# Row writes moved half a unit behind their transposes, and a unit's four loads issued together

## The chip, the cores and the metric

The kernel runs on one core of a Trainium2 chip. What counts is the device time of one execution in microseconds (us). Three timed runs of the kernel before gave 659.62, 659.68 and 662.8 us, so the median is 659.68 us.

## The reference: retention attention, then a mixture of experts

The inputs q, k and v have 8 batches, 8 heads, 576 positions and 64 values per head. The first half of the work is an attention without a softmax, whose scores decay with the distance of the two positions:

```
scores = matmul(q, k^T) / sqrt(64)
Dmat[i, j] = gamma_h ** (i - j) if i >= j else 0      # gamma_h = 1 - 2**(-5-h)
x = matmul(scores * Dmat, v)                          # 4608 tokens x 512
```

The second half routes the 4608 tokens to 8 experts. All token and expert logits (x @ w_gate) are sorted together, and the list is walked from the largest: a token goes to an expert that still has room, and an expert takes 576 tokens. Each expert then computes `relu(x @ w1[e]) @ w2[e]` for its own tokens.

## The kernel before

**Attention in 16 units.** A unit is one batch pair `bp` (4 of them) and one head pair `hp` (4 of them). Unit `u = 4*bp + hp` has 9 blocks of 128 positions, counted by a running step `g = 9*u + blk`. The loop at L769 works a unit in two halves, the first with blocks 0 to 3 and the second with 4 to 8. A half calls, in this order: `ahead(g)` for its blocks, the score matmuls of the next half (`A`, L551, with the mask multiply `am` on VectorE, L566), the state and value matmuls (`across`, `ST`, `within`), the eviction of the result to `xT` (`evict`, L628 on VectorE), and last the fills of its blocks, `fills(gs)`.

**Loads.** Each unit needs four tiles: `kin` and `qin` (k and q transposed), `vin` (v) and `nin` (k as it is). `load` (L505) issues them from the SP queue (L516). Each of the four names has three buffers, so the loads of unit u+2 need the buffers of unit u-1 free: k waits for TensorE's last score matmuls of unit u-1, q for the `across` matmuls at its end. The SP queue works in order: a DMA at its head that waits holds up everything behind it. `ahead` (L749) calls `load` for unit u+2.

**Scaling of v.** `vscale` (L543, L546) multiplies `vin` by powers of gamma in place on GpSimd (POOL), with two instructions for each unit, 512 and 640 columns wide. In the program it comes one unit ahead. POOL has nothing else to do in the attention, so it works as soon as a `vin` has landed.

**Fills.** What has to be done for a finished batch pair while the next one runs hangs on steps, by `at(g, f, ...)`: the router's logits (`logits`, `logits2`), the counts of the first search (`count_first`: tiles m, t, mx, oh and G on VectorE; `first_digits`: om, dg, DF and D; `first_table`: FT), and the copy of the attention's rows to the DRAM tensor `xd`, from which the experts' tokens are gathered later. For the first three batch pairs that copy is `rows` (L660): one VectorE transpose for each of 9 blocks (L665) into a tile `xr` that holds three blocks and has two buffers. After the third block of a tile four DMAs write it to `xd` (L670). The fourth batch pair's rows go another way (`rows_pe`, L685).

**After the attention.** The expert part begins with a search over the logits on VectorE and TensorE, then takes eight experts in turn. All of it hangs on the end of the attention.

Of the kernel before, what the change touches and what calls it, by code (L numbers as in the profile page):

```python
# [19 lines left out]
NP, HP, NB = 4, 4, 9  # L20
# [477 lines left out]
def attention(tc, nc, P, qk, vk, cst_d, wg_d, rf, xd, Lg):  # L498
# [6 lines left out]
    def load(u, what, cuts=None):  # L505

        bp, hp = divmod(u, HP)
        for i in what:
            n = 1024 if i == "n" else 1152
            t = P['ld'].tile([128, n], F32, name=i + "in", bufs=3)  # L510
            src = qk[bp, hp, "qk".index(i)] if i in "qk" else vk[bp, hp, :, :1152] if i == "v" else vk[bp, hp, :, 1152:]
            LD[u, i] = t
            if cuts:
                pieces[u, i] = [(t[:, a:b], src[:, a:b]) for a, b in zip((0,) + cuts, cuts + (n,))]
            else:
                nc.sync.dma_start(t, src)  # L516
# [19 lines left out]
    G = 16*NB  # L536
# [6 lines left out]
    def vscale(u, a, b):  # L543

        v = LD[u, 'v'][:, 128*a:128*b].rearrange("p (a d) -> p a d", d=64)
        nc.gpsimd.tensor_tensor(v, v, vs[:, u % HP, 2*a:2*b, None].to_broadcast([128, 2*(b-a), 64]), op=ALU.mult)  # L546
# [86 lines left out]
    def bank(shape, name):  # L633
        turn[0] += 1
        return P['bank'](tags[turn[0] % len(tags)], shape, name)
# [19 lines left out]
        c0 = bp*NB + b0  # L655
        nc.vector.tensor_reduce(Lg[:, c0:c0+n, :], pt[:, :n, :, 0:8].rearrange("p j h e -> p j e h"), axis=AX.X, op=ALU.add)

    TR = {}

    def rows(bp, blk):  # L660

        j = blk % 3
        if j == 0:
            TR[0] = P['w'].tile([128, 12, HP, 32], F32, name="xr", bufs=2)
        nc.vector.transpose(TR[0][:, 4*j:4*j+4].rearrange("p b h i -> p h b i"),  # L665
                            XT[bp][:, :, blk*128:(blk+1)*128].rearrange("p h (b i) -> p h b i", i=32))
        if j == 2:
            o = (bp*NB + blk - 2)*128
            for a in range(4):
                nc.sync.dma_start(xd[o:o+384, 128*a:128*a+128].rearrange("(b j) c -> j b c", j=32),  # L670
                                  TR[0][32*a:32*a+32].rearrange("p b h i -> p b (h i)"))

    def rows_pe(bp, blk, hps=range(HP)):

        if 0 in hps:
            TR[1] = bank([128, 512], "pT")
        pt = TR[1]
        for hp in hps:
# [18 lines left out]
    def at(g, f, *a):  # L697
        fill.setdefault(g, []).append((f, a))

    def rest(it):  # L700
        for _ in it:
            pass
    def both(a, b):
        while True:
            x, y = next(a, 0), next(b, 0)
            if x == y == 0:
                return
            yield
# [3 lines left out]
    for bp in range(NP):  # L712
        g0 = (bp+1)*4*NB + 2
        for k, b0 in enumerate((0, 3, 6)):
            if bp == NP-1 and k == 2:
                break
            g1 = g0 + 6*k if bp < NP-1 else G - NB + b0 + 3 + (1 if k == 0 else 0)
            c0 = bp*NB + b0
            at(g1, logits, bp, b0, b0+3)
            at(g1+4 if bp < NP-1 else g1+(1 if k == 0 else 2), logits2, bp, b0, b0+3)  # L720
            if bp == NP-1:
                it = R.count_first(c0, c0+3)
                if k == 0:
                    for i in range(6):
                        at(g1+2+i//2, next, it, None)
                else:
                    at(G-1, lambda it, k: rest(both(it, R.first_digits(27, 30) if k else iter(()))), it, k)
            elif k == 2:
                it = R.count_first(9*bp, 9*bp+9)
                for i in range(8):  # L730
                    at(g1+5+i//2, next, it, None)
                at(g1+13, lambda bp: R.count_first_pe([9*bp, 9*bp+3, 9*bp+6], bank), bp)
        if bp < NP-1:
            for blk in range(NB):
                at(g0 + (12 if bp < NP-2 else 10)*(blk//3) + 2*(blk%3) + 4, rows, bp, blk)
    for bp in range(3):
        g0, it = (bp+1)*4*NB + 2, R.first_digits(9*bp, 9*bp+9)
        for i in range(10):
# [10 lines left out]
    def ahead(g):  # L749

        u, blk = divmod(g, NB)
        if u + 2 < 16:
            if blk == 3:
                load(u + 2, "kq")
            if blk == 5:
                load(u + 2, "v")
            if blk == 6:
                load(u + 2, "n")
        if u + 1 < 16:
            if blk == 2:  # L760
                vscale(u + 1, 0, 4)
            if blk == 5:
                vscale(u + 1, 4, 9)
# [5 lines left out]
    for u in range(16):  # L769
        for hf in range(2):  # L770
            gs = range(NB*u + 4*hf, NB*u + 4 + 5*hf)
            for g in gs:
                ahead(g)
            if hf == 0 and u % HP == 0:
                XT[u//HP] = P['xt'].tile([128, HP, 1152], F32, name="xT")
            A(u + hf, 1 - hf)
            if hf == 0:
                A2(u)
            PX[u, hf] = two.tile([128, 2, 512], F32, name="pX", tag="X", bufs=1)
            across(u, (2, 3) if hf else (1,))  # L780
            ST(u, 1 + 2*hf)
            if u == 15 and hf:
                fills(gs[:1])
                gs = gs[1:]
            within(u, hf)
            ST(u + hf, 2 - 2*hf)
            if hf:
                within2(u)
                across(u, (4,))
            for c0, c1 in ((2, 3), (3, 4)) if u == 15 and hf else ((2*hf, 2*hf + 2),):  # L790
                evict(u, c0, c1)
            if hf:
                evict(u, 4, 5)
            fills(gs)
    P['close']()
    P['open']("pb")
    bp = NP-1
# [14 lines left out]
    c = R.first_digits(30, 36)  # L812
# [245 lines left out]
def build(tc, nc, qk, vk, cst, wg, rf, w1, w2, out):  # L1058
    with ExitStack() as top:
# [32 lines left out]
        with ExitStack() as ctx:  # L1092
            Q = dict(P)
            for name, bufs in (("a", 1), ("ld", 2), ("w", 2), ("xt", 2)):
                Q[name] = ctx.enter_context(tc.tile_pool(name="a_" + name, bufs=bufs))
            R, rows = attention(tc, nc, Q, qk, vk, cst, wg, rf, xd, Lg)

            def idle(what):

                if what in ("row", "rows"):  # L1100
                    if rows:
                        rows.pop(0)()
                    else:
                        warm(1)
                    what = 2*(what == "rows")
                if what:
                    warm(what)
            R.idle = idle
            run = moe(tc, nc, P, R, xd, w1, w2, out, mix)
            mix.drain(lambda: 0 in run.regs)  # L1110
            while rows:
                rows.pop(0)()
# [20 lines left out]
```

## Time and profile before

| what | value |
|---|---|
| median of three timed runs | 659.68 us |
| the profiled execution's own time | 656.27 us |
| its span, first to last instruction | 654.5 us |
| TensorE busy | 610.3 us (93%) |
| VectorE busy | 415.7 us (64%) |
| GpSimd busy | 179.2 us (27%) |
| mean granted TensorE clock | 0.987 of full speed |

The profile is of one execution. The span is its time between the first and the last instruction; the 1.8 us between it and 656.27 us lie around it. A busy share is an average over the whole span: the attention fills about the first 150 us of it, and the experts the rest. An idle time in brackets, as [2.30 <-DVE am L566], is how long the engine stood before the row and what released it. A row that begins with a time and has x2 or x4 is of so many instructions merged.

### The profile page before, as it was taken

The page shows a single profiled execution, that of the slowest core. Times are in us where ns is not written, and L with a number is a line of the kernel's source. Part 1 is how long each engine was busy: PE and PEld are TensorE (multiplying, and loading weights), DVE is VectorE, ACT ScalarE, POOL GpSimd, SP SyncE. Part 2 cuts the span into 40 slices and gives each one's busy share as a digit, 9 for nine tenths or more (in the row PEclk, how much of TensorE's full clock was granted, in tenths as well). Part 3 has the DMA queues.
Part 4 walks back from the last instruction along what each step waited for, and adds up shares of the span by engine and source line. Part 5 has one row for each costly group of instructions (what it writes and reads, how often), then busy time and mean ns, then how long its engine had stood idle before and what let it go on. Part 6 is the DMA issues. An engine that isn't in the chain of part 4 may idle for free.

```text
span 654.5 us, 14685 instructions
## 1 busy us (share of the span) xinstructions
PE 610.3 (93%) x5756; PEld 519.8 (79%) x5756; DVE 415.7 (64%) x1504; ACT 244.8 (37%) x424; POOL 179.2 (27%) x221
## 2 busy tenths in 40 slices
PE   8799897978868999999999999999999999999995
PEld 6677776765458877987997798789779889988984
DVE  3487969798855987887896799588774302311300
ACT  1111111113254344553455156235615734653511
POOL 2341122210221135134143141332314135131111
PEclk9999898999997999999999999999999999999999
DMA  9997898954379359789499568928966895893521
GB/s 337 401 388 230 270 344 272 335 174 146 129 192 219 67 187 248 177 233 240 136 227 230 167 161 209 242 89 204 227 191 155 188 277 153 195 244 117 98 64 40
DMA packets 51702, 134.19 MB, mean 205 GB/s; under 512 B 5810, under 2 KB 19762, under 8 KB 51634
## 3 DMA queue, kind: packets, MB, share of 16 engines
q1 hardware_dynamic: 36530, 81.08, 36.2%
q0 software_dynamic: 14960, 51.91, 35.9%
q8 instruction: 45, 0.74, 0.4%
q10 hardware_dynamic: 144, 0.26, 0.1%
q14 instruction: 23, 0.19, 0.1%
HBM read 81.33 MB, written 18.87 MB: 153 GB/s over the span
## 4 chain that ended last, share of the span: by engine, by line
PE 68%; DVE 15%; DMA 8%; issue 5%; ACT 1%; POOL 1%; SPq 1%; POOLq 0%; DVEq 0%; ACTq 0%
PE ph L961 26%; PE py L1000 24%; PE pA L564 4%; DMA qin<-in_qk 3%; PE pX L608 3%; PE pS L587 2%; PE pX L599 2%; DMA w1l<-raw 2%; PE pt L932 2%; PE r L332 2%; DMA w2l<-raw 1%; PE pT L641 1%; DMA cst<-in_cst 1%; DVE xr L665 1%; DVE am L566 1%
## 5 line engine op out<-in xcount | busy, mean ns | idle before, releaser
L1000 PE MATMUL py<-w2h,hb 128*128 128x512 f32 x576 | 188.2, 399 | 0.0
L961 PE MATMUL ph<-xh,w1l 128*128 128x320 f32 (+1 forms) x512 | 150.7, 298 | 6.0 <-DMA w1l<-raw 6.0
L961 PE MATMUL ph<-xh,w1h 128*128 128x320 f32 (+1 forms) x512 | 153.3, 303 | 2.5 <-ACT xh L934 1.8
L961 PE MATMUL ph<-xl,w1h 128*128 128x320 f32 (+1 forms) x512 | 150.6, 298 | 0.0
L1000 PE MATMUL py<-w2l,hb 128*128 128x512 f32 (+1 forms) x320 | 125.4, 392 | 0.2 <-DMA w2l<-raw 0.2
L1000 PEld LDWEIGHTS py<-w2h,hb 128*128 128x128 f32 x576 | 104.0, 188 | 20.6
L961 PEld LDWEIGHTS ph<-xh,w1l 128*128 128x128 f32 x512 | 97.4, 192 | 6.2 <-DMA w1l<-raw 6.2
L961 PEld LDWEIGHTS ph<-xh,w1h 128*128 128x128 f32 x512 | 97.3, 191 | 4.5 <-ACT xh L934 2.7
L961 PEld LDWEIGHTS ph<-xl,w1h 128*128 128x128 f32 x512 | 97.5, 192 | 0.6 <-DVE cs L336 0.3
L968 DVE SCALAR_TENSOR_TENSOR hb<-ph,hb 128x256 fp32r<-128x256 f32 (+1 forms) x192 | 59.1, 352 | 56.0 <-ACT hb L965 55.3
L965 ACT ACTIVATE hb<-ph 128x256 fp32r<-128x256 f32 (+1 forms) x128 | 52.4, 409 | 107.3 <-PE ph L961 107.3
L977 POOL DMA_INDIRECT out_y<-yt,idx x40 | 41.2, 1030 | 118.7 <-ACT yt L1017 76.6
L1000 PEld LDWEIGHTS py<-w2l,hb 128*128 128x128 f32 (+1 forms) x320 | 56.7, 177 | 13.8 <-DMA w2l<-raw 1.2
L546 POOL TENSOR_TENSOR vin<-vin,cst 128x512 f32<-128x512 f32 (+1 forms) x32 | 37.3, 1183 | 100.3 <-DMA vin<-in_vk 76.5
L906 POOL DMA_DIRECT2D w2l<-raw x32 | 28.9, 902 | 122.5 <-ACT hb L965 116.2
L589 ACT ACTIVATE S<-pS 128x128 f32<-128x128 f32 x64 | 17.8, 278 | 114.8 <-PE pS L587 114.8
L917 POOL DMA_INDIRECT xg<-xd,idx x40 | 41.5, 1037 | 70.3 <-DMA raw<-in_w 37.1
L1017 ACT ACTIVATE yt<-py 128x512 f32<-128x512 f32 x32 | 19.2, 598 | 105.8 <-PE py L1000 79.9
L564 PE MATMUL pA<-qin,kin 64*128 64x128 f32 x512 | 38.5, 289 | 13.4 <-DVE am L566 9.7
L566 DVE TENSOR_TENSOR am<-pA,cst 128x1024 f32<-128x1024 f32 x32 | 39.0, 1220 | 18.5 <-PE pA L564 18.3
L564 PEld LDWEIGHTS pA<-qin,kin 64*128 64x128 f32 x512 | 32.2, 191 | 22.8 <-DVE am L566 11.8
L1020 DVE TENSOR_TENSOR yt<-yt,py 64x512 f32<-64x512 f32 x8 | 5.4, 679 | 69.6 <-ACT yt L1019 69.5
(177 smaller groups left out, 889.9 us busy)
## 6 DMA issues: line engine op xcount, KB each, us to landing
raw<-in_w SPq DMA_DIRECT2D x64, 512.0 KB, 5.4
w2l<-raw POOLq DMA_DIRECT2D x32, 512.0 KB, 5.5
w1l<-raw POOLq DMA_DIRECT2D x31, 512.0 KB, 7.2
kin<-in_qk SPq DMA_DIRECT2D x14, 576.0 KB, 8.0
qin<-in_qk SPq DMA_DIRECT2D x14, 576.0 KB, 7.7
vin<-in_vk SPq DMA_DIRECT2D x14, 576.0 KB, 7.8
nin<-in_vk SPq DMA_DIRECT2D x14, 512.0 KB, 8.4
xd<-xr SPq DMA_DIRECT2D x36, 192.0 KB, 3.6
```

The source lines that it names most:

```text
L546: nc.gpsimd.tensor_tensor(v, v, vs[:, u % HP, 2*a:2*b, None].to_broadcast([128, 2*(b-a), 64]), op=ALU.mult)
L564: nc.tensor.matmul(pa[:, r, j], LD[u, 'k'][half(r), s], LD[u, 'q'][half(r), s], start=True, stop=True, skip_group_check=True)
L566: nc.vector.tensor_tensor(AM[u, hf], pa, m1[:, None, None, :].to_broadcast([128, 2, 4, 128]), op=ALU.mult)
L608: nc.tensor.matmul(PX[u, hf][half(h), b, 128*c:128*c+128], v[:, a:a+64], AM[u, hf][:, h ^ b, j], start=False, stop=False, skip_group_check ...
L906: nc.gpsimd.dma_start(lo, raw, accum_op=ALU.add)
L917: nc.gpsimd.indirect_dma_start(out=xg[:n, j, :], out_offset=None, in_=xd[:, :], in_offset=bass.IndirectOffsetOnAxis(ap=found[e][:n, j:j+1] ...
L961: T.matmul(ps, w, x, start=(k == 0), stop=(k == 11))
L965: A.activation(hb[:, f, c], ps, AF.Relu)
L968: V.scalar_tensor_tensor(hb[:, f, to+a:to+b], ps[:, a:b], 0.0, hb[:, f, 256*s+a:256*s+b].bitcast(F32), op0=ALU.max, op1=ALU.subtract)
L977: st = nc.gpsimd.indirect_dma_start(out=out[:, :], out_offset=bass.IndirectOffsetOnAxis(ap=found[e][:n, t:t+1], axis=0), in_=y[:n], in_off ...
L1000: T.matmul(ps[:m], a, w, start=(k == 0), stop=(k == last), skip_group_check=True)
L1017: A.activation(y, ps, AF.Copy)
```

## The change

The four DMAs that write a tile `xr` become a function of their own, `store`, hung six steps behind the tile's last transpose (and no later than the attention's last step). `ahead` issues all four loads of unit u+2 at a unit's first block, where it issued k and q at block 3, v at block 5 and n at block 6. `vscale` stays on GpSimd, at the steps where it was.

```diff
-    TR = {}
+    TR, TD = {}, {}
...
-        if j == 2:
-            o = (bp*NB + blk - 2)*128
-            for a in range(4):
-                nc.sync.dma_start(xd[o:o+384, 128*a:128*a+128].rearrange("(b j) c -> j b c", j=32),
-                                  TR[0][32*a:32*a+32].rearrange("p b h i -> p b (h i)"))
+        TD[bp, blk//3] = TR[0]
+
+    def store(bp, k):
+
+        o = (bp*NB + 3*k)*128
+        for a in range(4):
+            nc.sync.dma_start(xd[o:o+384, 128*a:128*a+128].rearrange("(b j) c -> j b c", j=32),
+                              TD[bp, k][32*a:32*a+32].rearrange("p b h i -> p b (h i)"))
...
-                at(g0 + (12 if bp < NP-2 else 10)*(blk//3) + 2*(blk%3) + 4, rows, bp, blk)
+                g1 = g0 + (12 if bp < NP-2 else 10)*(blk//3) + 2*(blk%3) + 4
+                at(g1, rows, bp, blk)
+                if blk % 3 == 2:
+                    at(min(g1 + 6, G - 1), store, bp, blk//3)
...
-        if u + 2 < 16:
-            if blk == 3:
-                load(u + 2, "kq")
-            if blk == 5:
-                load(u + 2, "v")
-            if blk == 6:
-                load(u + 2, "n")
+        if blk == 0 and u + 2 < 16:
+            load(u + 2, "kqvn")
```

Only the SP queue's order changes. On it, everything up to the q load of unit 7 stands as before. The first place is the SP queue around the first two row writes, those of batch pair 0. Before, with vin_817, vin_946 and vin_1079 (the next) the v tiles of units 7, 8 and 9:

```order
L516 DMA kin_759<-in_qk 128x1152
L516 DMA qin_761<-in_qk 128x1152
L670 DMA xd_65<-xr_748 32x12x128 x4
L516 DMA vin_817<-in_vk 128x1152
L516 DMA nin_820<-in_vk 128x1024
L516 DMA kin_880<-in_qk 128x1152
L516 DMA qin_882<-in_qk 128x1152
L516 DMA vin_946<-in_vk 128x1152
L516 DMA nin_949<-in_vk 128x1024
L670 DMA xd_65<-xr_933 32x12x128 x4
```

The write stood between the q and the v load of unit 7, so that v of unit 7 was the first load behind it and v of unit 8 the fifth. The same place on the SP queue now, where the v tiles of units 7, 8 and 9 are vin_762, vin_883 and vin_1015:

```order
L516 DMA vin_762<-in_vk 128x1152
L516 DMA nin_764<-in_vk 128x1024
L673 DMA xd_65<-xr_748 32x12x128 x4
L516 DMA kin_879<-in_qk 128x1152
L516 DMA qin_881<-in_qk 128x1152
L516 DMA vin_883<-in_vk 128x1152
L516 DMA nin_885<-in_vk 128x1024
L516 DMA kin_1011<-in_qk 128x1152
L516 DMA qin_1013<-in_qk 128x1152
L516 DMA vin_1015<-in_vk 128x1152
L516 DMA nin_1017<-in_vk 128x1024
L673 DMA xd_65<-xr_937 32x12x128 x4
```

The v and n loads of unit 7 have gone ahead of the write; behind it the third load is v of unit 8 and the seventh v of unit 9, and the next write has moved behind the loads of unit 9. The second place is the SP queue at the attention's end, with the last loads of the units 14 (vin_1710) and 15 (vin_1839) and the three writes of batch pair 2. Before:

```order
L670 DMA xd_65<-xr_1587 32x12x128 x4
L516 DMA kin_1654<-in_qk 128x1152
L516 DMA qin_1656<-in_qk 128x1152
L516 DMA vin_1710<-in_vk 128x1152
L516 DMA nin_1713<-in_vk 128x1024
L516 DMA kin_1781<-in_qk 128x1152
L516 DMA qin_1783<-in_qk 128x1152
L670 DMA xd_65<-xr_1770 32x12x128 x4
L516 DMA vin_1839<-in_vk 128x1152
L516 DMA nin_1842<-in_vk 128x1024
L670 DMA xd_65<-xr_1901 32x12x128 x4
L670 DMA xd_65<-xr_2028 32x12x128 x4
```

A write stood ahead of the last v load. The same place now, with the v tiles of units 14 (vin_1653) and 15 (vin_1784):

```order
L516 DMA qin_1651<-in_qk 128x1152
L516 DMA vin_1653<-in_vk 128x1152
L516 DMA nin_1655<-in_vk 128x1024
L673 DMA xd_65<-xr_1591 32x12x128 x4
L516 DMA kin_1780<-in_qk 128x1152
L516 DMA qin_1782<-in_qk 128x1152
L516 DMA vin_1784<-in_vk 128x1152
L516 DMA nin_1786<-in_vk 128x1024
L673 DMA xd_65<-xr_1770 32x12x128 x4
L673 DMA xd_65<-xr_1901 32x12x128 x4
L673 DMA xd_65<-xr_2028 32x12x128 x4
```

The last v load has moved ahead of that write, to the third load behind the write before it, and the three writes of batch pair 2 close the row.

## Rows read from the trace of the kernel before

**Rows 1.** The page's head

```profile
span 654.5 us, 14685 instructions
```

**Rows 2.** Busy us by engine in three stretches: PE, PEld, DVE, ACT, POOL, clock, DMA

```profile
60.30:73.00 12.70, 9.32 (x162) 7.88 (x158) 12.49 (x26) 1.39 (x5) 4.56 (x4) 0.87 0.85 294
...
98.10:110.30 12.20, 8.78 (x153) 7.45 (x151) 11.99 (x25) 1.11 (x4) 4.83 (x4) 0.86 0.77 272
...
134.70:146.30 11.60, 7.83 (x164) 6.65 (x160) 11.34 (x29) 1.39 (x5) 2.38 (x2) 1.00 0.44 127
```

**Rows 3.** SP queue's issues in order of time: start us, us, instruction

```profile
48.09 0.33 SPq L516 DMA_DIRECT2D qin<-in_qk  x1
53.62 2.57 SPq L670 DMA_DIRECT2D xd<-xr  x4
56.29 0.97 SPq L516 DMA_DIRECT2D vin<-in_vk  x1
...
79.21 2.85 SPq L670 DMA_DIRECT2D xd<-xr  x4
...
83.05 0.83 SPq L516 DMA_DIRECT2D qin<-in_qk  x1
```

**Rows 4.** PE in order of time: the end of unit 6, and a score matmul

```profile
64.22 0.30 PE L599 MATMUL pX<-qin,S 64*64 64x64 f32 x8
...
89.84 1.16 PE L564 MATMUL pA<-qin,kin 64*128 64x128 f32 x16 [0.61 <-DMA qin<-in_qk]
```

**Rows 5.** GpSimd's scalings of v in order of time

```profile
62.30 2.30 POOL L546 TENSOR_TENSOR vin<-vin,cst 128x512 f32<-128x512 f32 x2 [12.65 <-DMA vin<-in_vk]
68.83 2.26 POOL L546 TENSOR_TENSOR vin<-vin,cst 128x512 f32<-128x512 f32 x2 [4.23 <-PE pAt L575]
...
99.74 2.58 POOL L546 TENSOR_TENSOR vin<-vin,cst 128x512 f32<-128x512 f32 x2 [6.18 <-DMA vin<-in_vk]
105.68 2.26 POOL L546 TENSOR_TENSOR vin<-vin,cst 128x512 f32<-128x512 f32 x2 [3.36 <-DMA vin<-in_vk]
...
128.83 2.26 POOL L546 TENSOR_TENSOR vin<-vin,cst 128x512 f32<-128x512 f32 x2 [8.45 <-DMA vin<-in_vk]
136.47 2.38 POOL L546 TENSOR_TENSOR vin<-vin,cst 128x512 f32<-128x512 f32 x2 [5.38 <-DMA vin<-in_vk]
```

**Rows 6.** VectorE in order of time, beside a scaling

```profile
62.39 1.02 DVE L205 TENSOR_SCALAR m<-m 128x9 f32<-128x9 f32 x1
...
64.09 0.93 DVE L219 TENSOR_TENSOR G<-rc_f,m 128x384 bf16<-128x384 f32 x1
...
69.96 1.18 DVE L172 TENSOR_TENSOR dg<-dg,sm 128x45 int32<-128x45 int32 x1
...
101.12 1.28 DVE L209 TENSOR_TENSOR oh<-t,mx 128x72 bf16<-128x72 bf16 x1
...
105.83 0.92 DVE L151 TENSOR_SCALAR om<-m 128x9 int32<-128x9 int32 x1
106.78 1.18 DVE L153 TENSOR_TENSOR om<-m,om 128x9 int32<-128x9 int32 x1
...
136.73 0.92 DVE L201 TENSOR_TENSOR t<-t,decb 128x72 bf16<-128x72 bf16 x1
```

**Rows 7.** VectorE, the same instructions with no scaling beside them

```profile
62.28 0.20 DVE L201 TENSOR_TENSOR t<-t,decb 128x72 bf16<-128x72 bf16 x1
...
64.94 0.22 DVE L209 TENSOR_TENSOR oh<-t,mx 128x72 bf16<-128x72 bf16 x1
65.08 0.55 DVE L219 TENSOR_TENSOR G<-rc_f,m 128x384 bf16<-128x384 f32 x1
...
99.40 0.17 DVE L205 TENSOR_SCALAR m<-m 128x9 f32<-128x9 f32 x1
...
108.24 0.20 DVE L172 TENSOR_TENSOR dg<-dg,sm 128x45 int32<-128x45 int32 x1
...
142.39 0.17 DVE L153 TENSOR_TENSOR om<-m,om 128x9 int32<-128x9 int32 x1
```

## The prediction, made before the result was known

> **What bounds the kernel now.** I first cut the span [rows 1] into stretches with the table of busy time by window. Once the first loads are in, TensorE sets the pace of the attention, but for three stretches, one for each of the first three batch pairs, in which the router's counts and the row transposes fall on VectorE together: there VectorE is busy 12.49 of 12.70, 11.99 of 12.20 and 11.34 of 11.60 us, and TensorE only 9.32, 8.78 and 7.83 [rows 2]. So in these three stretches the end is set by VectorE, and TensorE stands idle 3.38 + 3.42 + 3.77 = 10.6 us. Everything after the attention hangs on its end, so a microsecond saved there is a microsecond of the whole.
>
> Then I read the SP queue in order of time, since that is all that the change reorders. It stands idle from 48.42 us, when the q load of unit 7 is out, to 53.62: the first row write waits for its transposes, and the v load of unit 7 gets out only at 56.29 [rows 3]. The same happens at 79.21: the write holds the loads of unit 10, whose q load goes out at 83.05 [rows 3], and TensorE, which wants it, starts its score matmul at 89.84 after 0.61 us of waiting for it [rows 4]. That 0.61 us is all that TensorE waits for a load behind a row write.
>
> The third view is GpSimd's timeline beside VectorE's. GpSimd scales v as soon as it lands, one pair of instructions of about 2.3 us a unit, and five of these pairs lie in the three stretches: at 62.30, 68.83, 99.74, 105.68 and 136.47 [rows 5]. Beside them short VectorE instructions are long: 1.18 us for a dg that takes 0.20 elsewhere, 1.28 for an oh of 0.22, 1.02 for an m of 0.17 [rows 6, 7]. The m that starts at 62.39 ends when the first half of the scaling does. Those that are long read and write SBUF alone, with one or two inputs; the mask multiplies and evictions, which read PSUM, and the transposes are not longer beside a scaling.
>
> **What the scalings cost there.** Row by row, blocked less free [rows 6, 7]. First stretch: m 1.02 - 0.17 = 0.85, G 0.93 - 0.55 = 0.38, two dg (one row shown, its twin before it 0.99) 0.79 + 0.98; sum 3.00. Second: a twin of that G 0.37, oh 1.06, om 0.92 - 0.17 = 0.75 and 1.18 - 0.17 = 1.01; sum 3.19. Third: t 0.92 - 0.20 = 0.72 and a last G (0.81) 0.26; sum 0.98. Together 7.17 us of the 10.6.
>
> **The change part by part.** No instruction is added or taken away: 36 write DMAs and the same loads, now in another order on SP.
>
> Loads ahead of the writes: q of unit 10 goes out when unit 7's q is free, before the write at 79.21 and so at least 3.8 us before 83.05. The wait of 0.61 goes; the bounds are 0 (something else of that matmul is late next) and 0.61, and I take 0.61, since the matmul's other input, k, is issued before q and VectorE is idle around it.
>
> Scalings: each moves with its v load. In before, v of unit 7 is the first load behind the first write and v of unit 8 the fifth, and they land at 62.3 and 68.8: 1.6 us a load [rows 3, 5]. Now unit 7's v is out at about 48.5 and lands near 54, where VectorE has gaps and nothing is lost. Behind the write stand v of unit 8 as the third load, near 62.3 + 2 x 1.6 = 65.6, and v of unit 9 as the seventh, near 72 (its q waits for the end of unit 6 at 64.2 [rows 4], which is not later than its turn). In the same way the pair at 99.74 and 105.68 becomes a third and a seventh load, near 102.7 and 108.7 in the old clock. At the other writes the third load was a v before and is one now, of the next unit, so those scalings stay in place. At the end the last v load stands third behind the write of the batch pair before, so the last scaling falls where the one at 128.83 was, and that of 136.47 is gone [rows 5]. Of five scalings in the stretches four are left, at new places.
>
> What they cost there, by laying them beside VectorE's order: from 65.6 to 67.9 VectorE, no longer held at 62.39, is at an am and two evictions, which read PSUM and run on, then at one G (about 0.5 lost) and an om (0.1 to 0.2). From 72 to 74.3 it is at the tables FT; some 0.7 is lost, of which the first idle time of VectorE behind the stretch takes a part. The second stretch gives the same, 0.5 and 0.5 to 1. Worked out so, about 2.3 are left. But a microsecond of error in a landing time puts a scaling on other instructions, and in before a scaling cost 7.17 / 5 = 1.43 on the mean. I take 0.8 for each, nearer to the laying out than to the mean: 3.2 left, 7.17 - 3.2 = 4.0 gained. The bounds: all four cost nothing, 7.17 gained; or each blocks VectorE for its whole 2.3, 9.2 in place of 7.17, a loss of 2.0.
>
> By the Trainium skill ("SBUF — State Buffer", section "SBUF: two separate sides") VectorE and GpSimd share one pair of ports as an exclusive lock: a GpSimd instruction and a VectorE instruction that has two SBUF inputs, or runs in a mode of two ports, block one another, and the first holds the pair for its whole length. The blocked rows agree, 1.18 in place of 0.20 beside a scaling, while a transpose between them was not longer. By that rule the sum would be between the 7.17 gained and the 2.0 lost, by what stands beside the scaling; it is the rule that makes the last rival possible.
>
> Writes six steps later: on SP they stand behind loads that wait for a unit's end, but that wait is over before or soon after their transposes are done (in before the second write waits for its transposes until 68.7, while unit 6 ends at 64.2 [rows 4]). Queued behind a waiting q load are its unit's v and n and then the write; who waits for a write is the transpose that takes the same xr buffer two tiles later, over a unit on, against a write whose issue takes 2.57 us [rows 3] and its landing. I cost it at nothing; if the cover were gone, VectorE would wait in its stretch, microsecond for microsecond. The last three writes have no load behind them and are out before the first gather.
>
> **Sum.** 0.61 + 4.0 = 4.6 us, of the profiled execution's 656.27: 651.7. That execution is 3.4 under the median of the timed runs; the same step from 659.68 gives 655.1.
>
> **The rivals.** A change of 0.5% is 3.3 us; less can't be told from no change.
> - *The scalings only trade places.* Four in the stretches cost what a scaling cost before, 1.43 each. Then only the fifth is saved: 7.17 - 5.7 + 0.6 = 2.1 us, 657.6, no change. For it speaks that the stretches hold many short instructions on SBUF alone; against it, that the third load falls on instructions that read PSUM.
> - *It doesn't do what it says for the time.* SP's waits were hidden but for 0.61, and VectorE's stretches follow the loads as they shift: 659.1, no change. For it: loads are needed a unit later than they are issued. Against it: GpSimd's starts are v's landings [rows 5].
> - *Slower: the scalings hit VectorE whole.* Four pairs in the stretches block VectorE 2.3 each, and a fifth slides from behind the second stretch onto the table instructions (FT) at its end: 5 x 2.3 = 11.5 against 7.17 + 0.61, 3.7 us more, 663.4. It decides for slower once the loss beside scalings passes 7.17 + 0.61 + 3.3 = 11.1. For it: 1.28 of 0.22 shows that an instruction can be held for a whole half. Against it: nowhere in before did a pair cost over 1.8.
>
> **How the numbers follow.** Forecast (gain over 3.3, up to 7.8) 0.57; trading places 0.29; nothing 0.06; slower 0.08. So faster 0.57, same 0.35, slower 0.08. The likeliest case's own range is 651.9 (all 7.8 gained) to 656.4. For 8 in 10 the range takes in the trade of places and the nothing, up to 660.5, and 651.5 below; the slower rival lies outside.
>
> **What would show it.** Right: the v load of unit 7 issued near 48.5 us; no wait of TensorE for qin at a score matmul after the attention's first quarter; no scaling after about 130 us; the rows dg, om and oh near 0.2 us, and the first two stretches 1.5 to 2.5 us shorter, the third 1. Wrong: the sum of long rows beside scalings unchanged near 7, or VectorE waiting for a write at a transpose. If the stretches are shorter and the whole is not, the step from the attention's end to the kernel's end is what failed.

## The result, and the profile of the changed kernel

The changed kernel takes 653.33 us in the median of four runs (651.54 to 654.29); the kernel before, run beside it, 661.08 (659.62 to 662.8). The ratio is 0.9879, with an interval of 0.9839 to 0.9918. That is faster by the 0.5% that the prediction set as its line, as forecast, and 653.33 lies in the range given. Two later sets of runs gave 0.9881 and 0.988. The gain of the medians is 7.8 us here, and 6.0 and 8.2 in the later sets, where the sum said 4.6, so the direction came out and a part of the sum was too small. The profiled execution of the changed kernel took 651.54 us against 656.27. The head of its page, which answers to [rows 1], is:

```profile
span 649.8 us, 14685 instructions
```

The span is 4.7 us shorter, with as many instructions.

The first place to look is the pace of the attention. I cut it at the end of the last VectorE eviction of units 6, 8, 10, 12, 14 and 16, so that each piece is the same work in each kernel. The first, third and fifth piece each hold one of the three VectorE stretches. The busy table of the kernel before, by these pieces (window; its length, then busy us of PE, PEld, DVE, ACT, POOL, with the instruction counts; granted clock, DMA share, GB/s):

```profile
57.47:77.64 20.17, 16.75 (x316) 14.52 (x314) 18.06 (x37) 2.67 (x9) 4.56 (x4) 0.92 0.89 285
77.64:94.44 16.80, 16.15 (x310) 12.32 (x308) 12.25 (x21) 3.26 (x11) 4.52 (x4) 1.00 0.96 326
94.44:114.93 20.49, 17.03 (x316) 14.70 (x314) 18.36 (x37) 2.67 (x9) 4.83 (x4) 0.92 0.87 292
114.93:131.92 16.99, 16.15 (x310) 12.31 (x308) 12.25 (x22) 3.25 (x11) 4.53 (x4) 1.00 0.98 336
131.92:150.58 18.66, 14.88 (x295) 11.80 (x293) 16.22 (x40) 2.88 (x9) 2.38 (x2) 1.00 0.51 151
```

The same pieces of the changed kernel:

```profile
57.72:75.61 17.89, 15.08 (x314) 13.10 (x314) 16.28 (x38) 2.67 (x9) 5.74 (x5) 1.00 1.00 342
75.61:91.83 16.22, 16.22 (x313) 12.43 (x312) 12.26 (x22) 3.25 (x11) 3.86 (x4) 1.00 1.00 341
91.83:109.81 17.98, 15.10 (x314) 13.12 (x314) 16.36 (x38) 2.67 (x9) 5.69 (x5) 1.00 1.00 334
109.81:126.01 16.20, 16.20 (x312) 12.41 (x312) 12.26 (x22) 3.26 (x11) 3.15 (x3) 1.00 1.01 346
126.01:143.65 17.64, 14.88 (x295) 11.79 (x293) 15.20 (x39) 2.88 (x9) 1.37 (x2) 1.00 0.33 78
```

Line by line the lengths fall by 2.28, 0.58, 2.51, 0.79 and 1.02 us, 7.18 in all. In the three stretches VectorE's busy time falls by 1.78, 2.00 and 1.02, that is 4.80 of their 5.81, though it runs the same instructions: they have become shorter. In the second and fourth piece VectorE's busy time is the same; there TensorE now fills the whole piece (16.22 of 16.22), where it stood 0.65 and 0.84 us before. The GpSimd column of the fifth piece falls from 2.38 to 1.37: only the tail of the last scaling is left in it, at its beginning.

Behind the attention stands a marker, the first reduce of the search (j, L251), before and after:

```profile
157.67 0.16 DVE L251 TENSOR_REDUCE j<-r 128x1 f32<-128x8 f32 x1
```

```profile
150.75 0.16 DVE L251 TENSOR_REDUCE j<-r 128x1 f32<-128x8 f32 x1
```

It comes 6.92 us earlier (7.18 less 0.25 by which unit 6 ended later). From there to the end of the span the kernel before took 654.5 - 157.67 = 496.8 us and the changed one 649.8 - 150.75 = 499.1, so this one execution gave 2.2 back behind the attention. The last experiments show that this does not belong to the change.

GpSimd's scalings, in order of time, answer to [rows 5]:

```profile
56.17 2.26 POOL L546 TENSOR_TENSOR vin<-vin,cst 128x512 f32<-128x512 f32 x2 [6.09 <-DMA vin<-in_vk]
65.83 2.58 POOL L546 TENSOR_TENSOR vin<-vin,cst 128x512 f32<-128x512 f32 x2 [7.40 <-DMA vin<-in_vk]
72.27 2.45 POOL L546 TENSOR_TENSOR vin<-vin,cst 128x512 f32<-128x512 f32 x2 [3.86 <-PE pA L564]
...
100.03 2.58 POOL L546 TENSOR_TENSOR vin<-vin,cst 128x512 f32<-128x512 f32 x2 [7.53 <-DMA vin<-in_vk]
106.45 2.44 POOL L546 TENSOR_TENSOR vin<-vin,cst 128x512 f32<-128x512 f32 x2 [3.85 <-PE pA L564]
...
125.12 2.26 POOL L546 TENSOR_TENSOR vin<-vin,cst 128x512 f32<-128x512 f32 x2 [5.88 <-PE pX L599]
```

Four lie in the first two stretches, none in the third, and none starts after 125.12. VectorE's rows beside the one at 65.83, and the first beside the one at 72.27, answer to [rows 6, 7]:

```profile
66.50 0.79 DVE L219 TENSOR_TENSOR G<-rc_f,m 128x384 bf16<-128x384 f32 x1
67.21 0.70 DVE L665 STREAM_TRANSPOSE xr<-xT 128x512 f32<-128x512 f32 x1
67.84 0.59 DVE L151 TENSOR_SCALAR om<-m 128x9 int32<-128x9 int32 x1
68.47 0.17 DVE L153 TENSOR_TENSOR om<-m,om 128x9 int32<-128x9 int32 x1
68.68 0.21 DVE L172 TENSOR_TENSOR dg<-om,sm 128x45 int32<-128x45 int32 x1
...
72.71 0.89 DVE L184 TENSOR_TENSOR FT<-k,D 128x512 bf16<-128x512 bf16 x1
...
76.16 0.38 DVE L184 TENSOR_TENSOR FT<-k,D 128x512 bf16<-128x512 bf16 x1
```

Three rows are still held: the G by 0.24 (free 0.55), an om by 0.42 (free 0.17) and an FT by 0.51 (free 0.38, the last row). The second om and the dg, which took 1.18 in [rows 6], take 0.17 and 0.21. The second stretch shows the same three at 0.86, 0.60 and 0.88. Together 2.4 us are lost, where it was 7.17.

The SP queue, which answers to [rows 3]:

```profile
48.76 1.03 SPq L516 DMA_DIRECT2D vin<-in_vk  x1
...
53.87 3.14 SPq L673 DMA_DIRECT2D xd<-xr  x4
...
74.72 0.35 SPq L516 DMA_DIRECT2D qin<-in_qk  x1
...
77.19 3.14 SPq L673 DMA_DIRECT2D xd<-xr  x4
...
108.91 0.35 SPq L516 DMA_DIRECT2D qin<-in_qk  x1
```

v of unit 7 goes out before the first write, at 48.76; q of unit 10 at 74.72 in place of 83.05, ahead of the write that held it. After 22 us TensorE waits for no load any more in the attention. The last row points at what the prediction overlooked. In the kernel before, q of unit 14 was held in the same way, behind the write of 116.50, and was issued at 120.34:

```profile
116.50 3.02 SPq L670 DMA_DIRECT2D xd<-xr  x4
...
120.34 0.88 SPq L516 DMA_DIRECT2D qin<-in_qk  x1
```

The score matmul that wants it waited 0.80 us, and the trace put that down to VectorE:

```profile
127.33 1.16 PE L564 MATMUL pA<-qin,kin 64*128 64x128 f32 x16 [0.80 <-DVE Lg L656]
```

A second profile of the same kernel (experiment 9) has that matmul again, with a longer wait and another name on it:

```profile
129.20 1.40 PE L564 MATMUL pA<-qin,kin 64*128 64x128 f32 x16 [1.99 <-DMA qin<-in_qk]
```

The name in the first profile misleads. That q landed 6.9 us after its issue, so near 127.24, just ahead of the matmul; and in the changed kernel the same matmul starts at 121.41, ahead of the same Lg at 122.06, so it does not need it. So there were two waits for q behind row writes, 0.61 and 0.80, and the change removes both.

### The profile page after: what moved, and what is told of

It is laid out like the page before. It is cut to its first block, busy times and chain, and to the rows that moved or that the text cites. A ratio compares the mean times of both kernels' runs of the same rounds, so it can differ in the third digit from the quotient of the medians.

```text
span 649.8 us, 14685 instructions
## 1 busy us (share of the span) xinstructions
PE 608.5 (94%) x5756; PEld 518.4 (80%) x5756; DVE 410.9 (63%) x1504; ACT 244.3 (38%) x424; POOL 178.5 (27%) x221
## 4 chain that ended last, share of the span: by engine, by line
PE 68%; DVE 16%; DMA 6%; issue 5%; ACT 2%; POOL 1%; SPq 0%; POOLq 0%; DVEq 0%; ACTq 0%
PE ph L962 25%; PE py L1001 25%; PE pA L564 3%; PE pX L608 3%; DMA qin<-in_qk 3%; PE pt L933 2%; PE pS L587 2%; PE r L332 2%; PE pX L599 2%; DVE am L566 1%; DMA w1l<-raw 1%; PE pT L641 1%; DVE G L163 1%; PE warm L1081 1%; DMA raw<-in_w 1%
```

## The experiments

The theory at this point: GpSimd's scalings hold VectorE in three stretches, and the change takes them off those places. The rival of the whole: it was the loads, or the writes, that TensorE or VectorE waited for. Each kernel of experiments 1 to 8 and 10 to 12 was timed beside the kernel before, whose medians were 659.58 (1 to 4), 659.05 (5 to 8) and 657.63 (9 to 12). Beside the times I use the lengths of the five pieces above.

**1 and 2. Each part alone.** Loads at the unit's first block, writes where they were:

```diff
-            if blk == 3:
-                load(u + 2, "kq")
-            if blk == 5:
-                load(u + 2, "v")
-            if blk == 6:
-                load(u + 2, "n")
+        if blk == 0 and u + 2 < 16:
+            load(u + 2, "kqvn")
```

> The four loads of a unit together, the writes where they were. Theory (scalings moved off the VectorE stretches, plus two waits of TensorE for q): units 7, 8, 12 and 15 are scaled as in the changed kernel, 9 and 13 come as third load behind their write, past the stretches; some 1.4 us are lost beside scalings in place of 7.2; the two q waits (1.4 us) stay; the search starts near 152, the kernel is 5 to 6 us faster than before. Rival (the gain is TensorE's, from loads that no longer stand behind a write): the writes of the third tile still hold k and q of units 10 and 14, so the search starts at 156 to 158 and the kernel gains 1 us or less.

Writes six steps later (in `store`, as in the change), loads where they were:

```diff
+                if blk % 3 == 2:
+                    at(min(g1 + 6, G - 1), store, bp, blk//3)
```

> The writes six steps later, the loads at blocks 3, 5 and 6. Theory: q of units 10 and 14 goes ahead of the write, both q waits go; v of units 9 and 13 is the first load behind a write and lands some 3 us later than in the changed kernel, still among the table rows; 7, 8, 12 and 15 are scaled as in the changed kernel; search near 151, 6 to 7 us faster than before. Rival (TensorE's loads alone): it has the whole gain as well, search near 151; the two runs with loads or writes alone then add up to the whole, where by the theory each has most of it.

The loads alone: 657.73 us, ratio 0.9959 (0.993 to 0.9988). The writes alone: 655.65, ratio 0.9913 (0.9878 to 0.9948). Neither is the whole: they gain 1.9 and 3.9 us, where the changed kernel gains 6.0 beside them (experiment 3). In the medians the two parts add up to the whole, which was to be the sign of the rival, and the loads alone start the search at 157.78, the place that the rival gave it and not 152. The writes alone start it at 156.75 and not 151. So this pair speaks against my theory as I had put it, and does not decide; experiments 5 and 6 do. The loads alone gain less than my theory gave them: the writes still hold the queue, and TensorE still waits 0.55 us for q of unit 10, as well as for an n:

```profile
88.80 1.16 PE L564 MATMUL pA<-qin,kin 64*128 64x128 f32 x16 [0.55 <-DMA qin<-in_qk]
...
131.20 0.45 PE L587 MATMUL pS<-vin,nin 128*64 128x64 f32 x8 [0.93 <-DMA nin<-in_vk]
```

The writes alone remove the q waits and empty the third stretch of scalings. In both, VectorE's loss beside scalings, summed by rows, falls, to 5.1 us (1.4 was expected) and 3.9, but the stretches do not follow it. Of the loads alone the third piece, of the writes alone the first:

```profile
93.39:114.89 21.50, 16.66 (x316) 14.44 (x314) 18.02 (x37) 2.67 (x9) 4.52 (x4) 0.92 0.90 300
```

```profile
58.41:78.80 20.39, 16.76 (x316) 14.63 (x314) 16.73 (x38) 2.66 (x9) 3.82 (x5) 0.92 0.95 311
```

In the last, VectorE is busy 16.73, close to the 16.28 of the changed kernel, yet the piece is 2.5 us longer. The granted clock of 0.92 points at the reason: for 3.4 us from 73.7 TensorE ran at 0.50, 1.2 GHz in place of 2.4, after a wait of 2.55 us where the changed kernel has 1.61. My theory had no term for that.

**3. The changed kernel again.**

> The changed kernel once more, for a second profile and as the yardstick of the others. In both theories the first reduction of the search starts near 150.8 us (157.7 before), the scalings of the units 8, 9, 12 and 13 stand in the VectorE stretches and cost about 2.4 us, and TensorE doesn't wait for a q load after unit 3. If the difference between the shorter attention (6.9 us) and the shorter span (4.7 us) is chance of the expert part, the expert part takes another time here, by some us; if the change itself lengthens it, it takes the 499.0 us of the first profile.

653.62 us, ratio 0.9881 (0.9838 to 0.9924). The profile differs from the first where it matters: the search starts at 154.11, and the first piece takes 21.54 us in place of 17.89. A scaling came at 66.72, 0.9 later than in the first profile (1.3 later measured from unit 6's end), and held both om, the second to 1.18:

```profile
66.72 2.26 POOL L546 TENSOR_TENSOR vin<-vin,cst 128x512 f32<-128x512 f32 x2 [7.74 <-PE pA L564]
```

```profile
67.83 1.18 DVE L153 TENSOR_TENSOR om<-m,om 128x9 int32<-128x9 int32 x1
```

TensorE then waited for the am behind them, and what it did next ran at half the clock:

```profile
71.38 2.08 PE L564 MATMUL pA<-qin,kin 64*128 64x128 f32 x16 [2.41 <-DVE am L566]
...
74.93 1.92 PE L608 MATMUL pX<-am,vin 128*64 128x128 f32 x16
```

The same two kinds of row take 1.16 and 1.05 at full clock. The table of that stretch:

```profile
70.80:77.60 6.80, 6.22 (x79) 5.55 (x80) 4.05 (x8) 0.49 (x2) 2.55 (x2) 0.50 0.69 227
```

VectorE, which had set the time until then, ran out of work:

```profile
73.64 1.21 DVE L566 TENSOR_TENSOR am<-pA,cst 128x1024 f32<-128x1024 f32 x1
77.93 0.89 DVE L628 TENSOR_TENSOR xT<-pX,cst 128x512 f32<-128x512 f32 x2 [3.08 <-PE pX L599]
```

So a stretch has a second price: if TensorE's clock falls in it and VectorE has not enough left to cover that, it costs more, about 3 us here, with 6.8 us at half the clock. In the kernel before the clock fell in the first two stretches too (0.92 above), but VectorE was busy 12.49 of 12.70 us around it [rows 2]. I take it to have been hidden there; that was not tested by itself.

**4. The second tile's transposes earlier.** The three transposes of the second tile of a batch pair come 7 steps behind the first's in place of 12 or 10, away from the count:

```diff
-                g1 = g0 + (12 if bp < NP-2 else 10)*(blk//3) + 2*(blk%3) + 4
+                g1 = g0 + (0, 7, 24 if bp < NP-2 else 20)[blk//3] + 2*(blk%3) + 4
```

> The changed kernel with the second tile's three transposes five steps earlier (7 steps behind the first tile's, not 12 or 10), out of the VectorE stretches. Theory (VectorE's order in the stretch sets the time): each stretch loses up to 3 x 0.63 = 1.9 us, so the search starts 3 to 5.6 us earlier than in the changed kernel, near 146, and the kernel is that much faster. Rival (TensorE's own work or loads bound the attention by now): the search starts near 150 and the time is that of the changed kernel.

650.57 us, ratio 0.984 (0.9797 to 0.9882), 3 us under the changed kernel. The first piece takes 16.58 and the fifth 16.78, against 17.89 and 17.64; the third took 19.05, with 3.4 us at half clock from 103.4. So the search starts at 149.57, near the rival's 150 and not at 146: two pieces became shorter as the theory said, and the third lost it again.

**5 and 6. No scaling.** The scalings of units 6 to 15 are left out, in the kernel before and in the changed one:

```diff
-        nc.gpsimd.tensor_tensor(v, v, vs[:, u % HP, 2*a:2*b, None].to_broadcast([128, 2*(b-a), 64]), op=ALU.mult)
+        if u < 6:
+            nc.gpsimd.tensor_tensor(v, v, vs[:, u % HP, 2*a:2*b, None].to_broadcast([128, 2*(b-a), 64]), op=ALU.mult)
```

> The kernel before, with v of the units 6 to 15 left unscaled (GpSimd does nothing from about 45 us to the attention's end), so its numbers are not the reference's. Theory (time is lost where a scaling holds VectorE): the 7.2 us beside scalings go, the two q waits stay, so the search starts near 150.5 in place of 157.7; this kernel and the changed one without scalings then differ by the q waits alone, 1 to 2.5 us. Rival (loads behind writes cost the time): the search still starts at 155 to 158, and the two kernels without scalings differ by nearly the whole 6.9 us.

> The changed kernel with v of the units 6 to 15 left unscaled. Theory: only the 2.4 to 3.0 us that are still lost beside scalings go; the search starts near 148, and no stretch has TensorE at 1.2 GHz since VectorE no longer keeps it waiting over 2 us. Rival: the search starts 5 us or more earlier than in the kernel before without scalings.

The kernel before without them: 650.74 us, ratio 0.9878 (0.985 to 0.9906). The search starts 5.9 us earlier, 1.2 later than the theory's 150.5 and well ahead of the rival's 155 to 158:

```profile
151.73 0.16 DVE L251 TENSOR_REDUCE j<-r 128x1 f32<-128x8 f32 x1
```

The pieces with the three stretches:

```profile
57.61:74.80 17.19, 15.43 (x316) 13.26 (x314) 15.08 (x38) 2.66 (x9) 0.00 (x0) 1.00 0.92 292
...
92.34:109.81 17.47, 15.38 (x316) 13.25 (x314) 15.19 (x37) 2.66 (x9) 0.00 (x0) 1.00 0.90 301
...
126.98:144.62 17.64, 15.10 (x295) 11.80 (x293) 15.20 (x39) 2.87 (x9) 0.00 (x0) 1.00 0.57 161
```

VectorE's busy time is 15.08, 15.19 and 15.20. The kernel before had 2.98 + 3.17 + 1.02 = 7.17 more, which is the sum that the prediction had made row by row (3.00, 3.19, 0.98); the pieces were 2.98, 3.02 and 1.02 longer. The changed kernel has 1.20 + 1.17 + 0 = 2.37 more. That settles the main step: the whole excess of VectorE's busy time was the scalings, and the change removes two thirds of it. With the scalings the two falls of the clock went as well (1.00 in all three pieces).

The changed kernel without scalings: 646.83, ratio 0.9823 (0.979 to 0.9855). That is 3.9 us under the kernel before without them although no scaling is left to move, more than the 1 to 2.5 of the theory and less than the rival's 6.9. There the moved loads and writes show without the scalings: the unscaled kernel before waits 0.99 us for a q and 0.92 and 0.83 for two n, the changed one for none, and its second and fourth piece take 16.13 and 16.41 in place of 17.54 and 17.17, 2.2 us together. The rest of the 3.9 is not assigned; of the 3.7 us between the two profiles 2.1 lie behind the start of the search. Two forecasts for this kernel failed: its fifth piece took 19.21 for 17.64, with 3.4 us at half clock from 138.4 where no fall was expected, so the search starts at 150.10 and not at 148.

**7 and 8. Dummy matmuls ahead of the counts.** To test the clock, TensorE is given six matmuls of 128x512, whose results nobody reads, just before the first count's matmuls of each stretch (`warm` takes the tile for them from `bank`):

```diff
+                at(g1+13, P['warm'], 6, bank)
                 at(g1+13, lambda bp: R.count_first_pe([9*bp, 9*bp+3, 9*bp+6], bank), bp)
```

> The changed kernel with six dummy matmuls (some 1.3 us) on TensorE in each stretch, ahead of the count matmuls, where it waits for VectorE. Theory (of the spread between runs of the changed kernel, 650.8 to 655.2, the larger part is that TensorE falls to 1.2 GHz after its second wait in a stretch: 2.41 us of waiting and 6.8 us at 1.2 GHz in the second profile, none in the first): no fall in the stretches, search near 150.5 in every profile, the median 1 to 2 us below the changed kernel's 653.6. Rival (the spread is the expert part's): the same median as the changed kernel, or up to 1 us more for the dummy matmuls.

And the same with the earlier transposes of experiment 4:

> The second tile's transposes early, with the six dummy matmuls. Theory: in the run without them TensorE was at 1.2 GHz for 3.4 us in the second stretch (from 103.4); that goes; search near 147 in place of 149.6, the median 1 to 2.5 us below 650.6. Rival: 650.6 or a little more.

646.58 us, ratio 0.9822 (0.9792 to 0.9851), and 644.27, ratio 0.9783 (0.9755 to 0.981). These are 7.0 and 6.3 under experiments 3 and 4, far more than forecast, but on another chip. The dummies lie in the time that TensorE would have stood; the wait for the am behind them is 0.87 us:

```profile
69.09 1.47 PE L1082 MATMUL warm<-full 128*128 128x512 bf16 x6
70.39 0.37 PE L231 MATMUL cnt<-oh,G 128*128 128x8 bf16 x9
71.64 1.16 PE L564 MATMUL pA<-qin,kin 64*128 64x128 f32 x16 [0.87 <-DVE am L566]
```

No piece of either kernel has a granted clock under 1.00. But the first piece takes 18.45, more than the changed kernel's 17.89 where its clock did not fall, and 17.73 against 16.58 with the earlier transposes. The searches start at 151.26 and 149.63, where 150.5 and 147 were forecast. So these profiles show the fall gone and no shorter attention than one without a fall.

**9 to 12. One chip for all.** These are the kernel before and those of experiments 3, 7 and 8 once more. Open were whether the distance between the changed kernel and the dummies was one of chips, and whether the 2.2 us lost behind the attention belong to the change.

> The kernel before, looked at once more, beside the three below. If the stretch of the fourth expert (56.05 us between its VectorE rows in the first profile of before, 58.9 to 60.4 in five profiles of kernels with the loads or stores moved, 56.0 in four others) goes with the kernel, it takes 56.0 here; if it goes with the job or by chance, it takes 58.9 here as well, or another value of its own. The scalings of v cost VectorE 6 to 8 us in the three stretches, the search starts 157 to 158 us after the span's start.

> The changed kernel a third time. The theory (scalings hold VectorE, and TensorE's fall to 1.2 GHz at the end of a stretch decides how much of the rest is seen): 650 to 654, ratio 0.985 to 0.99; the search starts at 150 to 151 where no fall at half clock is seen in a stretch, about 154 where one is. Rival (the fall has nothing to do with it): the search starts at 151 with or without a fall.

> The changed kernel with six dummy matmuls ahead of the first count of each stretch, on the same chip as the changed kernel itself. The theory: no stretch at 1.2 GHz between 60 and 150 us, 4 to 7 us under the changed kernel (645 to 648). Rival, that the earlier distance was one of chips: within 2 us of the changed kernel.

> The changed kernel with the second tile's transposes seven steps behind the first's, and the dummy matmuls. If both edits hold on one chip: 643 to 646, 2 to 3 us under the dummy matmuls alone, 6 to 9 under the changed kernel. Rival, that the two edits take the same microseconds: no different from the dummy matmuls alone.

The kernel before, one run: 660.34 us, a search at 162.72 where 157 to 158 was expected. Its five pieces took 20.62, 16.76, 20.79, 19.73 and 20.28: the fourth holds the wait of 1.99 for q of unit 14, and the clock fell in the fourth and fifth as well, so the attention took 5 us longer than in the first profile. VectorE is busy 8.0 us longer in its five pieces than in those of experiment 5, where it was 7.2 in the first profile. The changed kernel: 649.45 us, ratio 0.988 (0.9837 to 0.9922), search at 152.4, no fall in any piece, and a first piece of 17.86. The search is later than the 150 to 151 forecast for a profile without a fall; unit 6 had ended 1.3 later. Measured from unit 6's end the search came after 93.0 and 93.4 us in the two profiles of the changed kernel without a fall, and after 96.8 in the one with it. That speaks against the rival, that the fall has nothing to do with it, by one profile with a fall.

With the dummies: 646.81, ratio 0.9825 (0.9786 to 0.9864), 2.6 us under the changed kernel on the same chip, between the 4 to 7 of the theory and the rival's 2. The attention of this profile is no shorter than that of the changed kernel's (93.7 against 93.4 from unit 6's end), as it must be where neither had a fall; its span is 1.2 shorter, and that lies behind the start of the search (493.1 against 494.8). So it does not show where the 2.6 come from. What fits the theory is the spread of the six runs, 647.63 to 652.6 without and 645.27 to 647.79 with, but that a run at 652.6 had a fall is not shown, since only one execution of each is profiled. With the earlier transposes as well: 645.6, ratio 0.9821 (0.9777 to 0.9864). It is 1.2 us under the dummies alone, less than the 2 to 3 expected, and not told from them here. It is 3.9 under the changed kernel, with one of its six runs (649.33) among those of the changed kernel and five below all of them. So the last kernel beats the kernel before and the changed one; that it beats the dummies alone is not shown.

The time behind the attention: the stretch of the fourth expert, between two additions to yt on VectorE, took 60.4 us in the first profile of the changed kernel, 58.9 in experiment 3, and 56.0 in experiment 10 (first the changed kernel's first profile, then the one of experiment 10):

```profile
425.67 0.68 DVE L1021 TENSOR_TENSOR yt<-yt,py 64x512 f32<-64x512 f32 x1
...
486.05 0.67 DVE L1021 TENSOR_TENSOR yt<-yt,py 64x512 f32<-64x512 f32 x1
```

```profile
428.30 0.68 DVE L1021 TENSOR_TENSOR yt<-yt,py 64x512 f32<-64x512 f32 x1
...
484.31 0.67 DVE L1021 TENSOR_TENSOR yt<-yt,py 64x512 f32<-64x512 f32 x1
```

It is the same program three times, so these 4 us are no part of the change. The kernel before took 56.05 and 56.3 in its two profiles, the second on the chip where the changed kernel took 56.0. All four kernels of experiments 1 to 4, which ran on one chip, took 58.9, and all four of 5 to 8, on another, 56.0; what makes the difference stays open.

## Why the prediction was right, and where its sum was short

- *VectorE sets the time in three stretches, and scalings hold it there.* Right, and the size too: 7.17 us by rows, 7.17 by taking the scalings away.
- *Each scaling moves with its load.* Right. The places forecast were 65.6 and 72, and 102.7 and 108.7 in the old clock; they came at 65.83 and 72.27, and at 100.03 and 106.45 in a clock that by then ran 2.6 us early. The scaling of unit 7 came at 56.17, not near 54, and held nothing. The scaling at the third stretch went. The rows at 72.27 and 106.45 name TensorE as what released them, but they start 7.0 and 7.1 us after their v loads were issued (65.26 and 99.36), and loads of v took 5.8 to 9.4 us to land in the kernel before, so the landing fits as well.
- *What the four cost at their new places.* The step that was mis-sized. Laid out beside VectorE's order it was 2.3 us, on G, om and FT; measured 2.37, on G, om and FT. I took 3.2, towards the mean of before, and so 4.0 of gain in place of 4.80. The laying out was the better number, in part by luck: its total fits, its rows do not. In the first stretch it had the G at 0.5, the om at 0.1 to 0.2 and the FT at 0.7; measured are 0.24, 0.42 and 0.51. One sign of being right, om near 0.2, failed with that. It was also not safe: 0.9 us later, as in experiment 3, a scaling held both om.
- *The wait for q.* Right for unit 10, 0.61. The second, 0.80 for unit 14, was missed, because I looked only for rows that named a load. That is 0.79 of the shortfall by the fourth piece.
- *The stretches.* The first two were to be 1.5 to 2.5 us shorter and the third 1: they are 2.28, 2.51 and 1.02 shorter. About 0.5 us of each of the first two is VectorE standing less (2.11 to 1.61, and 2.13 to 1.62), for which the sum had no term; which wait went there I have not told apart, and the fall of TensorE's clock in these pieces of before is one candidate.
- *The sum.* 4.80 + 1.01 + 1.37 = 7.18 us in the attention, against 4.0 + 0.61. The profiled executions differ by only 4.7, near the forecast, but that is chance: 0.25 was lost ahead and 2.2 behind. The gains of the three pairs of medians, 7.8, 6.0 and 8.2, lie nearer to the attention's 7.2 than to the forecast.
- *The rivals.* Trading places would have left 5.7 us of loss, and 2.4 are left. Hitting VectorE whole did not come: no held row is over 0.9 (in experiment 3 one is 1.18). The later writes cost nothing in this profile: no transpose waits for one.
- *Not in the sum at all.* TensorE at half clock. It bears on the slower rival: with a shift of about a microsecond in one scaling the first piece was 3.7 us longer (experiment 3). Over several runs the gain stands, ratio 0.988 three times, but a single profile could have told another story.

By the Trainium skill ("SBUF — State Buffer", section "SBUF: two separate sides") the shared pair of ports is an exclusive lock, held for a whole instruction. The traces agree: a G that takes 0.55 was held to 0.79, while a transpose in the middle of the same scaling took its usual 0.70, and with no scaling at all the whole of the 7.17 us is gone.

## What to carry to other kernels

Where one engine's short instructions run long at certain places, sum them by rows against free rows of the same instruction, find what runs beside them, and move that by moving what releases it, here the loads. When the new places can be laid out row by row, trust that sum over the mean of the old places, but add a margin for a shift of a microsecond. Before counting waits for a load, follow each load from its issue to the instruction that first reads it, rather than look for rows that name it.

## What the runs showed that I had not expected

- *The clock fell in the middle of a busy kernel.* TensorE ran at 1.2 GHz for 3.4 or 6.8 us at a time. Within the five pieces this was seen in seven of the ten profiles without dummy matmuls, and in none of the four with them. The wait ahead of it, or around its start, was 2.41, 2.48, 2.55 and 2.64 us in four of the cases and 1.87 in experiment 4, but a wait of 2.16 was twice not followed by a fall (experiments 2 and 10), and one of 1.69 in the fifth piece was followed by one in experiments 2 (at 145.4), 6 (at 138.4) and 9 (at 150.4) but not in the changed kernel, so the length of the wait does not tell it alone. In that piece 3.4 us at 1.2 GHz went with some 1.6 us more: 20.28 for 18.66 in the kernel before, 19.21 for 17.64 without scalings.
- *Removing one wait uncovers another.* Late loads cost the kernel before 1.4 us; with the scalings left out they cost it 0.99 + 0.92 + 0.83 = 2.7.
- *The name on a wait can be wrong.* The wait for q of unit 14 was put down to VectorE in one profile (0.80 us) and to its DMA in the next (1.99).
